# Sliding-window attention and a gated mixture of experts: token blocks of 256 by seven products of quarters in both layers

## The chip, the cores and the metric

The kernel runs on one core of one Trainium2 chip, in fp32. The metric is the time of one execution on the device in microseconds; the number for a kernel is the median of several executions. Matmuls run on TensorE (PE in the profile, its weight loads PEld), elementwise work on VectorE (DVE), ScalarE (ACT) and GpSimd (POOL), and SyncE (SP) issues most of the DMAs.

## What is computed

Eight sequences of 576 tokens pass through attention with eight heads of 64 and a causal window of 64 positions. The heads are joined to rows of 512 numbers, and each of the 4608 rows goes through one of eight experts, a two-layer network with a hidden width of 1024. The expert is the largest of eight gate logits, or the previous token's expert where a local gate says so. Cut to what matters:

```python
scores = np.where(mask, q @ k.T / 8, -1e9)             # mask: 0 <= i - j < 64
x = (softmax(scores) @ v).transpose(0, 2, 1, 3).reshape(B, S, 512)
for b in range(B):
    prev_e = -1
    for s in range(S):
        fresh_e = int(np.argmax(logits[b, s]))
        e = fresh_e if s == 0 or local_gate[b, s] < 0.5 else prev_e
        prev_e = e
        h = np.maximum(x[b, s] @ w1[e], 0.0)             # 512 -> 1024
        out[b, s] = p[e] * (h @ w2[e])                   # 1024 -> 512, p: softmax of the logits
```

## The kernel before, in words

**Attention** (`attention`) works in nine stretches of 512 tokens and four pairs of heads. PE makes the scores and the products with the values, ACT the exponentials, DVE masks them (L276) and divides. Rows go to a DRAM tensor `xs`. The logits come out of the same products.

**The router** (`Router`) sorts tokens by expert into blocks on the chip. `first` handles the first 1728 tokens and fills six whole blocks of 128 tokens while attention still runs; `second` handles everything that is left, 3840 tokens, while those six blocks run. Its tables hold the token of each place (`idx`), its factor (`pw`) and each block's expert (`ej`). Before, the rest is cut into 8 big blocks of 256 tokens, 14 small ones of 128 and 4 half blocks of 64, whose numbers are fixed when the kernel is built; a branch at the end (`more`) handles blocks beyond them.

**The experts** (`Experts`) take one block after the other, in an order that `run` writes out: the six first blocks, then big ones, with a half block after each second one, then the small blocks, and a half block last. For each block:

- `rows` gathers the token rows by an indirect DMA from POOL's queue (L922), `weights` loads both weight matrices of its expert, 2 MB each, from SP's queue (L934). Both are issued two blocks ahead. The weights go into a ring of four buffers (`ring`), and every third block's into two spare ones.
- `turn` transposes the rows on PE (L947) and copies them out of PSUM (L948), on ACT for the six first blocks and on DVE for the rest.
- `hidden` is layer 1: for each of 8 slices of 128 hidden numbers, 4 matmuls with a 128x128 piece of `w1` standing in the array and the block's tokens moving (L962). Each piece of PSUM then goes through a ReLU into `h`, by turns on ACT (L968) and DVE (L966).
- `result` is layer 2: for each 128 tokens, 8 matmuls with a piece of `h` standing and 512 columns of `w2` moving (L992), a copy with the factor on ACT (L997), and an indirect DMA to the output (L998).

On PE the program order is `hidden` of a block, `turn` of the next, `result` of the block. PE's order is written out by hand (`manual_schedule`); the other engines' order in this stage is left to the scheduler. The trace has two records for each fp32 matmul of the program: a big block's layer 1 has 32 matmuls and 64 records.

Of the kernel before, what the change touches and what calls it, by code (L numbers as in the profile page):

```python
# [19 lines left out]
P = 128  # L20
# [26 lines left out]
SMALL = LEFT - NB * BIG  # L47
HF = P // 2
NSM = (SMALL + E * (HF - 1)) // P
SURE = SMALL // P, E // 2  # L50
NBLK = NB + NSM + E
HF0 = SM0 + NSM
NS = HF0 + E
NEG = -1.0e9
SC = 4 * P
NSC = N // SC
# [89 lines left out]
def attention(ctx, tc, ring, q, k, v3, vt, xs, lt, ok, wg2, ident, rt, ex):  # L146
# [49 lines left out]
    col = cp.tile([P, KB, WIN], I32, name="col")  # L196
    nc.gpsimd.iota(col, pattern=[[0, KB], [1, WIN]], base=0, channel_multiplier=0)
    colf = cp.tile([P, KB, WIN], F32, name="colf")
    nc.vector.tensor_copy(colf, col)
    masks = []  # L200
    for i in range(2):
# [322 lines left out]
class Router:  # L524
# [295 lines left out]
    def second(self, psum):  # L820
# [13 lines left out]
        vec.tensor_scalar(bend, bend, float(NB), None, Alu.min)  # L834
        vec.tensor_scalar(boff, boff, float(NB), None, Alu.min)
        vec.tensor_tensor(nb, bend, boff, op=Alu.subtract)

        lim = tl("lim", P, E)
        vec.tensor_scalar(lim, nb, float(BIG), None, Alu.mult)
# [40 lines left out]
        vec.tensor_tensor(pl, pl, self.oh, op=Alu.mult)  # L880
        lo, hi = self.places(pl, CV)
        ej = tabs["ej"]
        self.experts_of(ej[:, :NBLK], NBLK, [(NB, bend), (NSM, send), (E, hend)])
        more = tl("more", 1, 1)
        vec.tensor_scalar(more, hend[0:1, E - 1:], float(SURE[1]), None, Alu.is_gt)
        vec.scalar_tensor_tensor(ej[:, NBLK:], send[0:1, E - 1:], float(SURE[0]), more, Alu.is_gt, Alu.max)
        yield 6.0, False
        at = yield from self.table(psum, slice(0, CV), NS, lo, hi, tabs["idx"], tabs["pw"])

# [2 lines left out]
            vec.tensor_copy(tabs["pwh"][i * HF:(i + 1) * HF], tabs["pw"][:HF, HF0:])  # L892


class Experts:


    def __init__(self, ctx, tc, ring, xs, w1, w2, out, tabs, lt, ident):
        self.tc, self.nc, self.ring, self.spare = tc, tc.nc, ring, None
# [4 lines left out]
    def fetch(self, n, spare=False):  # L904

        st = self.rows({}, n)
        return self.weights(st, n, spare)

    def rows(self, st, n):
        tabs = self.tabs  # L910
        if n < 0:
            idx, pw, rows = tabs["idx1"], tabs["pw1"], T1
            slots = range(-1 - n, -n)
        else:
            idx, pw, rows = tabs["idx"], tabs["pw"], N + 1
            slots = range(2 * n, 2 * n + 2) if n < NB else range(SM0 + n - NB, SM0 + n - NB + 1)
        st.update(x=[], slots=slots, idx=idx, pw=pw, rows=P)
        if n >= NB + NSM:
            st.update(half=n - NB - NSM, rows=HF)
        for s in slots:  # L920
            x = (self.xp if n < 0 else self.xq).tile([P, D], F32, name="xg")
            self.nc.gpsimd.indirect_dma_start(  # L922
                out=x, out_offset=None, in_=self.xs[:rows, :],
                in_offset=bass.IndirectOffsetOnAxis(ap=idx[:, s:s + 1], axis=0))
            st["x"].append(x)
        return st

    def weights(self, st, n, spare=False):
# [12 lines left out]
    def turn(self, st, quiet):  # L941
        nc, n = self.nc, st["rows"]
        st["xt"] = xt = self.wk.tile([P, DK, BIG], F32, name="xt")
        for i, x in enumerate(st["x"]):
            tp = self.ps_t.tile([P, DK, P], F32, name="tp")
            for kk in range(DK):
                nc.tensor.transpose(tp[:, kk, :n], x[:n, kk * P:(kk + 1) * P], self.ident[:n, :n])  # L947
            (nc.scalar.copy if quiet else nc.vector.tensor_copy)(xt[:, :, i * P:i * P + n], tp[:, :, :n])  # L948

    def hidden(self, st, quiet, step):  # L950
        nc = self.nc
        n = len(st["slots"]) * st["rows"]
        st["h"] = h = self.wk.tile([P, FK, BIG], F32, name="h")
        each = 512 // n
        for g in range(FK // each):
            hp = self.ps_h.tile([P, each, n], F32, name="hp")
            for i in range(each):
                m = g * each + i
                for kk in range(DK):
                    for f in range(0, P, st["rows"]):  # L960
                        a = slice(f, f + st["rows"])
                        nc.tensor.matmul(hp[a, i, :], lhsT=st["w1"][:, kk, m * P:(m + 1) * P][:, a],  # L962
                                         rhs=st["xt"][:, kk, :n], start=(kk == 0), stop=(kk == DK - 1))
            o = h[:, g * each:(g + 1) * each, :n]
            if (g % 2 or "half" in st) and not quiet:
                nc.vector.tensor_relu(o, hp)  # L966
            else:
                nc.scalar.activation(o, hp, Act.Relu)  # L968
            step()

    def result(self, st, step):
        nc = self.nc
        if "half" in st:

            s, w = st["half"], D // 2
# [13 lines left out]
        for i, s in enumerate(st["slots"]):  # L989
            yp = self.ps_y.tile([P, D], F32, name="yp")  # L990
            for m in range(FK):
                nc.tensor.matmul(yp, lhsT=st["h"][:, m, i * P:(i + 1) * P], rhs=st["w2"][:, m, :],  # L992
                                 start=(m == 0), stop=(m == FK - 1))
                if m == FK // 2 - 1:
                    step()
            y = self.wk.tile([P, D], F32, name="y")
            nc.scalar.activation(y, yp, Act.Copy, scale=st["pw"][:, s:s + 1])  # L997
            nc.gpsimd.indirect_dma_start(  # L998
                out=self.out[:, :], out_offset=bass.IndirectOffsetOnAxis(ap=st["idx"][:, s:s + 1], axis=0),
                in_=y, in_offset=None, bounds_check=N - 1, oob_is_err=False)  # L1000
            step()

    def space(self, ctx):
        tc = self.tc
        self.spare = ctx.enter_context(tc.tile_pool(name="ex_spare", bufs=2))
# [6 lines left out]
    def run(self, ctx, rt, last=None):  # L1012
# [5 lines left out]
        jobs, late = self.jobs, []  # L1018

        def psum():  # L1020
            return ps_r.tile([P, SC], F32, name="r")

        side = rt.second(psum)

        pause = 0.0

        def step():
# [5 lines left out]
            while side and not trip:  # L1033
                w, trip = next(side, (0.0, None))
                pause += w
                if trip is None:
                    side = None
                    late.append(self.fetch(0, spare=True))

        order = [-1 - n for n in range(FIRST)]  # L1040
        halves = list(range(NB + NSM, NB + NSM + SURE[1]))
        for n in range(NB):
# [4 lines left out]
        total = len(order)  # L1047
        self.turn(jobs[0], True)
        step()
        for i in range(total):  # L1050
            quiet = i < FIRST
            n = order[i + 2] if i + 2 < total else 0
            if n:
                jobs.append(self.fetch(n, spare=n > 0 and (i + 2 - FIRST) % 3 == 0))
            self.hidden(jobs[i], quiet, step)
            if i == FIRST - 1:
                while side:
                    step()
                jobs.insert(FIRST, late[0])
                if last:  # L1060
                    last(psum())
            if i + 1 < total:
                self.turn(jobs[i + 1], quiet)
            self.result(jobs[i], step)

    def more(self, ctx):

        self.space(ctx)
        for i, n in enumerate([*range(NB + SURE[0], NB + NSM), *range(NB + NSM + SURE[1], NBLK)]):
            st = self.fetch(n, spare=i % 3 == 2)  # L1070
# [44 lines left out]
```

## Time and profile before

| | |
|---|---|
| median of three runs | 716.15 us (715.06 to 717.1) |
| the profiled execution's own time | 716.17 us |
| its span, from the first to the last instruction | 714.4 us |
| mean granted TensorE clock | 0.988 |
| PE busy in the span | 667.7 us (93%) |
| DVE busy | 188.5 us (26%) |
| ACT busy | 127.3 us (18%) |
| POOL busy | 117.5 us (16%) |
| first big block starts, last matmul ends | 242.65 us, 705.85 us |

A group's row in the view by lines gives the time in which any of its instructions ran, their mean length, and behind the bar the time in which the engine stood idle before them. Matmuls overlap, so their mean length is longer than the distance between their starts; in the view in order of time, a run's distance is read from the start of one row to the start of the next.

### The profile page before, as it was taken

Reading aid. Unit: us, or ns where it says so; the run is one execution under the profiler, and the core shown is the slowest. Engines: PE = TensorE matmul, PEld = TensorE weight load, DVE = VectorE, ACT = ScalarE, POOL = GpSimd, SP = SyncE. Lnnn points to the kernel's source line nnn. Section 1 sums busy time; section 2 is a strip of 40 time slices with the busy share of each in tenths; the row PEclk is TensorE's granted clock in tenths of the full one; section 3 lists DMA queues with packets and bytes.
Section 4 is the critical chain, followed back from the end, with each engine's and each line's share of the span. In section 5 each row is a group of like instructions: output and inputs, shape, how many; then the busy total and the mean of one; then the engine's idle time right before and its main releaser. Section 6 shows DMA issues by size and latency. Waiting matters only on the chain. (4 is left out here: it accounts for less than half of the span.)

```text
span 714.4 us, 13220 instructions
## 1 busy us (share of the span) xinstructions
PE 667.7 (93%) x5796; PEld 485.8 (68%) x5796; DVE 188.5 (26%) x451; ACT 127.3 (18%) x182; POOL 117.5 (16%) x128
## 2 busy tenths in 40 slices
PE   4888886889999999999999999999999999999994
PEld 2666665776777767585767658676767776677663
DVE  5666896766640010011011001110100001000100
ACT  2655554421111101000010100011001100011000
POOL 4311112211222210112021112101111111010001
PEclk9999999999999999999999999999999999999998
DMA  8999998999879983585567548545988989888700
GB/s 309 388 384 363 393 355 297 401 359 352 325 263 405 407 322 133 205 341 189 227 226 298 197 147 352 214 147 212 327 322 327 323 335 319 327 293 327 266 15 19
DMA packets 37428, 203.85 MB, mean 285 GB/s; under 512 B 3529, under 2 KB 3551, under 8 KB 29168
## 3 DMA queue, kind: packets, MB, share of 16 engines
q1 hardware_dynamic: 28544, 173.45, 65.8%
q0 software_dynamic: 8816, 29.45, 10.4%
q8 instruction: 48, 0.79, 0.4%
q14 instruction: 20, 0.16, 0.1%
HBM read 184.01 MB, written 19.40 MB: 285 GB/s over the span
## 5 line engine op out<-in xcount | busy, mean ns | idle before, releaser
L962 PEld LDWEIGHTS hp<-xt,w 128*128 128x128 f32 (+1 forms) x2304 | 258.3, 179 | 28.9 <-issue 14.7
L962 PE MATMUL hp<-xt,w 128*128 128x128 f32 (+2 forms) x2304 | 274.6, 287 | 1.2 <-ACT xt L948 1.2
L992 PE MATMUL yp<-w,h 128*128 128x512 f32 x576 | 252.7, 593 | 0.0
L992 PEld LDWEIGHTS yp<-w,h 128*128 128x128 f32 x576 | 107.1, 190 | 123.7 <-issue 122.2
L966 DVE TENSOR_SCALAR h<-hp 128x512 f32<-128x512 f32 x34 | 23.5, 691 | 424.8 <-issue 282.8
L998 POOL DMA_INDIRECT out_dram<-y,idx x36 | 37.4, 1040 | 271.9 <-ACT y L997 243.4
L997 ACT ACTIVATE y<-yp,pw 128x512 f32<-128x512 f32 x36 | 24.7, 687 | 317.0 <-PE yp L992 310.7
L922 POOL DMA_INDIRECT xg<-xs,idx x40 | 41.0, 1026 | 193.8 <-PE tp L947 150.6
L257 PE MATMUL sp<-w 64*64 64x128 f32 (+1 forms) x1296 | 48.1, 284 | 14.0 <-DMA w<-in_q_dram 7.2
L257 PEld LDWEIGHTS sp<-w 64*64 64x64 f32 x1296 | 41.5, 146 | 26.6 <-issue 12.0
L286 PE MATMUL xo<-vb,p 128*64 128x74 f32 x576 | 47.9, 236 | 11.3 <-issue 7.2
L276 DVE TENSOR_TENSOR p<-p,mask 128x1024 f32<-128x1024 f32 x36 | 45.9, 1274 | 25.0 <-ACT p L273 25.0
L968 ACT ACTIVATE h<-hp 128x512 f32<-128x512 f32 x42 | 25.1, 597 | 150.7 <-PE hp L962 150.7
L286 PE MATMUL xo<-va,p 128*64 128x74 f32 x576 | 47.7, 236 | 4.1 <-issue 3.5
L286 PEld LDWEIGHTS xo<-vb,p 128*64 128x64 f32 x576 | 41.5, 141 | 13.2 <-issue 6.7
L273 ACT ACTIVATE p<-sp 128x1024 f32<-128x1024 f32 x36 | 36.9, 1025 | 55.4 <-PE sp L257 55.2
L286 PEld LDWEIGHTS xo<-va,p 128*64 128x64 f32 x576 | 41.5, 141 | 7.1 <-issue 6.4
L233 POOL COPY vb<-va 64x1184 f32<-64x1184 f32 x9 | 11.0, 1217 | 93.3 <-PE xo L286 72.5
L295 DVE TENSOR_TENSOR x<-xo,allr 128x512 f32<-128x512 f32 x36 | 24.5, 680 | 0.0
L947 PE MATMUL tp<-ident,xg 128*128 128x128 f32 (+1 forms) x160 | 22.4, 271 | 0.0
L948 DVE COPY xt<-tp 128x512 f32<-128x512 f32 (+1 forms) x32 | 20.1, 647 | 0.0
L947 PEld LDWEIGHTS tp<-ident,xg 128*128 128x128 f32 (+1 forms) x160 | 17.8, 140 | 2.0 <-issue 1.0
(222 smaller groups left out, 235.0 us busy)
## 6 DMA issues: line engine op xcount, KB each, us to landing
w<-in_w_dram SPq DMA_DIRECT2D x64, 2048.0 KB, 9.2
va<-in_v_dram SPq DMA_DIRECT2D x9, 1184.0 KB, 12.7
vtt<-in_vt_dram SPq DMA_DIRECT2D x9, 1024.0 KB, 7.7
xs<-x POOLq DMA_DIRECT2D x9, 1024.0 KB, 10.3
w<-in_k_dram SPq DMA_DIRECT2D x17, 512.0 KB, 11.2
w<-in_q_dram SPq DMA_DIRECT2D x17, 512.0 KB, 12.2
xg<-xs,idx POOLq DMA_INDIRECT x40, 8.9
out_dram<-y,idx POOLq DMA_INDIRECT x36, 8.3
```

The source lines that it names most:

```text
L257: nc.tensor.matmul(sp[c * WIN:(c + 1) * WIN, j, a:b], lhsT=kt[h, hp, block * WIN:(block + 1) * WIN], rhs=qt[h, hp, a:b], start=True, stop= ...
L273: nc.scalar.activation(p, sp, Act.Exp, scale=DH ** -0.5)
L276: nc.vector.tensor_tensor(p, p, m.to_broadcast([P, 2, SC]), op=Alu.mult)
L286: nc.tensor.matmul(xo[par * WIN:(par + 1) * WIN, j, s * VW:(s + 1) * VW], lhsT=p[:, j, b * WIN:(b + 1) * WIN], rhs=w[:, s, 2 * hp + j, :], ...
L295: nc.vector.tensor_tensor(x[:, :, hp].rearrange("p c j d -> p j c d"), o[:, :, :, :DH], rr.to_broadcast([P, 2, 4, DH]), op=Alu.mult)
L922: self.nc.gpsimd.indirect_dma_start(out=x, out_offset=None, in_=self.xs[:rows, :], in_offset=bass.IndirectOffsetOnAxis(ap=idx[:, s:s + 1], ...
L947: nc.tensor.transpose(tp[:, kk, :n], x[:n, kk * P:(kk + 1) * P], self.ident[:n, :n])
L962: nc.tensor.matmul(hp[a, i, :], lhsT=st["w1"][:, kk, m * P:(m + 1) * P][:, a], rhs=st["xt"][:, kk, :n], start=(kk == 0), stop=(kk == DK - 1))
L968: nc.scalar.activation(o, hp, Act.Relu)
L992: nc.tensor.matmul(yp, lhsT=st["h"][:, m, i * P:(i + 1) * P], rhs=st["w2"][:, m, :], start=(m == 0), stop=(m == FK - 1))
L997: nc.scalar.activation(y, yp, Act.Copy, scale=st["pw"][:, s:s + 1])
L998: nc.gpsimd.indirect_dma_start(out=self.out[:, :], out_offset=bass.IndirectOffsetOnAxis(ap=st["idx"][:, s:s + 1], axis=0), in_=y, in_offse ...
```

## The change

Every block of 256 tokens is computed by Strassen's scheme in both layers. A product of two matrices cut in quarters is made of seven products of quarters, or of sums of quarters, in place of eight. `left` makes the four sums of one operand and `right` those of the other, on DVE; `product` is one of the seven, accumulated in PSUM. What two results share stays in PSUM while ACT copies it aside (`keep`), and DVE adds the copy to the finished half (`relu` in layer 1, `put` in layer 2).

- In layer 1 a product is 8 matmuls with 128 moving columns, in place of 32 matmuls with 256 for the whole block; in layer 2 it is 4 matmuls with 256 moving columns, in place of 16 with 512.
- The sums of the weights (`ws1`, `ws2`), of the tokens (`xs`) and of the hidden numbers (`hs`) are made anew for every block, 16 instructions.
- The tokens are cut differently: 13 big blocks, 4 small and 4 half ones. A half or small block follows each second big one; one big, one small and one half block end the order.
- The spare weight buffers go; all weights use the ring of four. `h` has one buffer.
- From the fifth first block on, the order of DVE and ACT is the program's too. The router has to be done one block earlier.
- The router's table has 48 columns in place of 41.

The core of the diff:

```diff
-NB = -(-(LEFT - E * (BIG - 1)) // BIG)
+NB = (LEFT + E * (HF - 1)) // BIG
+SURE = (LEFT + E * HF) // BIG - E // 2, E // 2, E // 2
...
-        self.shifted(nb, cnt, 0, BIG.bit_length() - 1)
+        self.shifted(nb, cnt, HF - 1, BIG.bit_length() - 1)
...
         for name, w, a, b in (("w1", self.w1, DK, F), ("w2", self.w2, FK, D)):
-            t = (self.spare if spare else self.ring).tile([P, a * b], F32, name="w")
+            t = self.ring.tile([P, a * b], F32, name="w")
...
+        if st["big"]:
+            st["xq"] = quarters(xt, DK, BIG)
+            st["xt"] = self.right("xs", st["xq"])
+            w = quarters(st["w1"], DK, F)
+            st["wq"] = [[w[0][0], w[1][0]], [w[0][1], w[1][1]]]
+            st["ws"] = self.left("ws1", st["wq"])
+
+    def left(self, name, a):
+        sub, add = Alu.subtract, Alu.add
+        s1, s2, s3, s4 = self.sums(name, a)
+        for o, x, y, op in ((s1, a[1][0], a[1][1], add), (s2, s1, a[0][0], sub), (s3, a[0][0], a[1][0], sub),
+                            (s4, a[0][1], s2, sub)):
+            self.nc.vector.tensor_tensor(o, x, y, op=op)
+        return s1, s2, s3, s4
...
+    def big_hidden(self, st):
+        a, s, b, t = st["wq"], st["ws"], st["xq"], st["xt"]
+        st["w2q"] = w2 = quarters(st["w2"], FK, D)
+        st["w2t"] = self.right("ws2", w2)
...
+        def product(out, a, b, start=True, stop=True):
+            for m in range(n):
+                for kk in range(DK // 2):
+                    nc.tensor.matmul(out[:, m, :], lhsT=a[:, kk, m * P:(m + 1) * P], rhs=b[:, kk, :],
+                                     start=start and m + kk == 0,
+                                     stop=stop and (m, kk) == (n - 1, DK // 2 - 1), skip_group_check=True)
...
+        product(px, a[0][0], b[0][0], stop=False)
+        u = keep(0, px)
+        product(py, s[0], t[0], stop=False)
+        z = keep(1, py)
+        product(px, s[1], t[1], False, False)
+        v = keep(2, px)
+        product(pz, a[0][1], b[1][0])
+        relu(hq[0][0], pz, u)
+        product(px, s[2], t[2], False, False)
+        relu(hq[1][1], px, z)
+        product(py, s[3], b[1][1], False)
+        relu(hq[0][1], py, v)
+        product(px, a[1][1], t[3], False)
+        relu(hq[1][0], px)
+        st["ha"] = [[hq[0][0], hq[1][0]], [hq[0][1], hq[1][1]]]
+        st["hs"] = self.left("hs", st["ha"])
+
+    def big_result(self, st):
...
+        product(px, a[0][0], b[0][0], stop=False)
+        u = keep(0, px, pw[0])
+        product(py, s[0], t[0], stop=False)
+        z = keep(1, py, pw[1])
+        product(px, s[1], t[1], False, False)
+        v = keep(2, px, pw[0])
+        product(pz, a[0][1], b[1][0])
+        put(0, 0, pz, u)
+        product(px, s[2], t[2], False, False)
+        put(1, 1, px, z)
+        product(py, s[3], b[1][1], False)
+        put(0, 1, py, v)
+        self.scatter(st, 0, y[0])
+        product(px, a[1][1], t[3], False)
+        nc.scalar.activation(y[1][:, :w], px, Act.Copy, scale=pw[1])
+        self.scatter(st, 1, y[1])
...
+        small = list(range(NB, NB + SURE[1]))
+        half = list(range(NB + E, NB + E + SURE[2]))
+        between = half[1:] + small
+        for n in range(SURE[0]):
             order.append(n)
-            if n % 2 and len(halves) > 1:
-                order.append(halves.pop(0))
-        order += list(range(NB, NB + SURE[0])) + halves
+            if n % 2 and between:
+                order.append(between.pop(0))
+        order += between + half[:1]
```

On PE, where the big blocks begin, the program before has one row for each layer of a block (`hp` is layer 1's PSUM tile, `yp` layer 2's, `tp` that of the transposes of the next block's rows `xg`; `64x64` rows are a half block):

```order
L962 MATMUL hp<-xt,w 128x256 x32
L947 MATMUL tp<-ident,xg 128x128 x8
L992 MATMUL yp<-w,h 128x512 x16
L962 MATMUL hp<-xt,w 128x256 x32
L947 MATMUL tp<-ident,xg 128x64 x4
L992 MATMUL yp<-w,h 128x512 x16
L962 MATMUL hp<-xt,w 64x64 x64
L947 MATMUL tp<-ident,xg 128x128 x8
L979 MATMUL yp<-w,h 64x256 x16
```

After, the first big block at the same place on PE (`xs` and `ws` are the sums of tokens and weights, `hs` those of the hidden numbers; both layers' PSUM tiles are called `hp`):

```order
L998 MATMUL hp<-xt,w 128x128 x8
L998 MATMUL hp<-xs,ws_2840 128x128 x16
L998 MATMUL hp<-xt,w 128x128 x8
L998 MATMUL hp<-xs,ws_2840 128x128 x8
L998 MATMUL hp<-xt,ws_2840 128x128 x8
L998 MATMUL hp<-xs,w 128x128 x8
L947 MATMUL tp<-ident,xg 128x128 x8
L1041 MATMUL hp<-w,h 128x256 x4
L1041 MATMUL hp<-ws_2868,hs 128x256 x8
L1041 MATMUL hp<-w,h 128x256 x4
L1041 MATMUL hp<-ws_2868,hs 128x256 x4
L1041 MATMUL hp<-w,hs 128x256 x4
```

Layer 1 is now 56 matmuls with 128 columns, and layer 2 is 28 with 256, the seventh product following the last row. Five of the seven products read a sum.

DVE in the same place before, where each pair of ReLUs belongs to one big block and the copies to the next block's transposed rows:

```order
L966 TENSOR_SCALAR h<-hp 128x512 x2
L948 COPY xt<-tp 128x4x128 x2
L966 TENSOR_SCALAR h<-hp 128x512 x2
L948 COPY xt<-tp 128x4x64
L966 TENSOR_SCALAR h<-hp 128x8x64
```

DVE after, between the two layers of the first big block, with the rows of the second one being prepared (`kept` are ACT's copies of layer 2, `y` the rows for the output):

```order
L948 COPY xt<-tp 128x4x128 x2
L971 TENSOR_TENSOR xs<-xt 128x256
L971 TENSOR_TENSOR xs<-xt,xs 128x256
L971 TENSOR_TENSOR xs<-xt 128x256
L971 TENSOR_TENSOR xs<-xt,xs 128x256
L963 TENSOR_TENSOR ws_2969<-w 128x1024
L963 TENSOR_TENSOR ws_2969<-ws_2969,w 128x1024
L963 TENSOR_TENSOR ws_2969<-w 128x1024
L963 TENSOR_TENSOR ws_2969<-w,ws_2969 128x1024
L1050 SCALAR_TENSOR_TENSOR y<-hp,pw,kept_2983 128x256
L1050 SCALAR_TENSOR_TENSOR y<-hp,pw,kept_2989 128x256
L1050 SCALAR_TENSOR_TENSOR y<-hp,pw,kept_2995 128x256
```

The sums for the next block's first layer now stand on DVE ahead of the three instructions that finish this block's second layer. After these rows come four more weight sums (128x1024), three additions and four sums of hidden numbers (128x512 each).

More of the change, by code (lines that the diff above doesn't have):

```diff
@@ L892, in second, with quarters @@
             vec.tensor_copy(tabs["pwh"][i * HF:(i + 1) * HF], tabs["pw"][:HF, HF0:])
+def quarters(t, rows, cols):
+    r, c = rows // 2, cols // 2
+    return [[t[:, i * r:(i + 1) * r, j * c:(j + 1) * c] for j in range(2)] for i in range(2)]
 class Experts:
     def __init__(self, ctx, tc, ring, xs, w1, w2, out, tabs, lt, ident):
-        self.tc, self.nc, self.ring, self.spare = tc, tc.nc, ring, None
+        self.tc, self.nc, self.ring = tc, tc.nc, ring
         self.xs, self.w1, self.w2, self.out, self.tabs, self.ident = xs, w1, w2, out, tabs, ident
@@ L916, in rows @@
             slots = range(2 * n, 2 * n + 2) if n < NB else range(SM0 + n - NB, SM0 + n - NB + 1)
-        st.update(x=[], slots=slots, idx=idx, pw=pw, rows=P)
-        if n >= NB + NSM:
-            st.update(half=n - NB - NSM, rows=HF)
+        st.update(x=[], slots=slots, idx=idx, pw=pw, rows=P, big=len(slots) == 2)
+        if n >= NB + E:
+            st.update(half=n - NB - E, rows=HF)
         for s in slots:
@@ new lines, in big_result, with product, keep, put @@
+    def big_result(self, st):
+        nc = self.nc
+        a, s, b, t = st["ha"], st["hs"], st["w2q"], st["w2t"]
+        w = D // 2
+        px, py, pz = (self.ps_h.tile([P, D], F32, name="hp")[:, :w] for _ in range(3))
+        pw = [st["pw"][:, i:i + 1] for i in st["slots"]]
+        y = [self.wk.tile([P, D], F32, name="y") for _ in range(2)]
+        def product(out, a, b, start=True, stop=True):
+            for m in range(FK // 2):
+                nc.tensor.matmul(out, lhsT=a[:, m, :], rhs=b[:, m, :], start=start and m == 0,
+                                 stop=stop and m == FK // 2 - 1, skip_group_check=True)
+        def keep(i, x, pw):
+            o = self.one.tile([P, w], F32, name=f"kept{i}")
+            nc.scalar.activation(o, x, Act.Copy, scale=pw)
+            return o
+        def put(i, j, x, y2):
+            nc.vector.scalar_tensor_tensor(y[i][:, j * w:(j + 1) * w], x, pw[i], y2, Alu.mult, Alu.add)
+        product(px, a[0][0], b[0][0], stop=False)
[14 more added lines that the diff above has]
+        self.scatter(st, 1, y[1])
@@ L950, in hidden, with scatter @@
+    def scatter(self, st, i, y):
+        s = st["slots"][i]
+        self.nc.gpsimd.indirect_dma_start(
+            out=self.out[:, :], out_offset=bass.IndirectOffsetOnAxis(ap=st["idx"][:, s:s + 1], axis=0),
+            in_=y, in_offset=None, bounds_check=N - 1, oob_is_err=False)
     def hidden(self, st, quiet, step):
         nc = self.nc
-        n = len(st["slots"]) * st["rows"]
-        st["h"] = h = self.wk.tile([P, FK, BIG], F32, name="h")
+        if st["big"]:
+            return self.big_hidden(st)
+        n = st["rows"]
+        st["h"] = h = self.wk.tile([P, FK, BIG], F32, name="h", bufs=1)
@@ L988, in result @@
             return
[L989 to L1001, printed above, removed]
+        yp = self.ps_y.tile([P, D], F32, name="yp")
+        for m in range(FK):
+            nc.tensor.matmul(yp, lhsT=st["h"][:, m, :P], rhs=st["w2"][:, m, :], start=(m == 0), stop=(m == FK - 1))
+            if m == FK // 2 - 1:
+                step()
+        y = self.wk.tile([P, D], F32, name="y")
+        nc.scalar.activation(y, yp, Act.Copy, scale=st["pw"][:, st["slots"][0]:st["slots"][0] + 1])
+        self.scatter(st, 0, y)
+        step()
     def space(self, ctx):
         tc = self.tc
-        self.spare = ctx.enter_context(tc.tile_pool(name="ex_spare", bufs=2))
+        self.one = ctx.enter_context(tc.tile_pool(name="ex_one", bufs=1))
         self.xq = ctx.enter_context(tc.tile_pool(name="ex_xq", bufs=6))
```

79 lines of the change are left out of this document (46 added, 33 removed).

## The prediction

> **What bounds the kernel now.** I read the page's busy times first, then the groups by line with shapes kept apart, then PE in order of time, then the stage's window, and last the rows of DVE, POOL and the DMA queue that have to price the new work.
>
> ```profile
> PE 667.7 (93%) x5796; PEld 485.8 (68%) x5796; DVE 188.5 (26%) x451; ACT 127.3 (18%) x182; POOL 117.5 (16%) x128
> ...
> L992 PE MATMUL yp<-w,h 128*128 128x512 f32 x576 | 252.7, 593 | 0.0
> ...
> L962 PE MATMUL hp<-xt,w 128*128 128x128 f32 x1280 | 146.7, 275 | 1.2 <-ACT xt L948 1.2
> L962 PE MATMUL hp<-xt,w 128*128 128x256 f32 x512 | 112.1, 380 | 0.0
> ```
>
> PE does nearly all of the work and almost never waits in the experts' stage: the idle time ahead of its three large groups is 1.2 us in all. From the first big block to the last matmul nothing else counts:
>
> ```profile
> core 0: us, PE busy (x) PEld busy (x) DVE busy (x) ACT busy (x) POOL busy (x), PEclk, DMA share, GB/s
> 242.65:705.85 463.20, 462.35 (x2657) 325.24 (x2655) 41.55 (x66) 40.65 (x64) 59.54 (x60) 1.00 0.69 254
> ```
>
> PE is busy for 462.35 of 463.20 us at a granted clock of 1.00, DVE for 41.55 us. So a shorter PE program shortens this stage one for one, until an engine that now idles is late. In PE's order of time:
>
> ```profile
> 213.20 7.31 PE L962 MATMUL hp<-xt,w 128*128 128x128 f32 x64
> 220.34 0.60 PE L947 MATMUL tp<-ident,xg 128*128 128x128 f32 x4
> 220.78 7.03 PE L992 MATMUL yp<-w,h 128*128 128x512 f32 x16
> ...
> 242.65 13.98 PE L962 MATMUL hp<-xt,w 128*128 128x256 f32 x64
> 256.46 1.04 PE L947 MATMUL tp<-ident,xg 128*128 128x128 f32 x8
> 257.33 13.90 PE L992 MATMUL yp<-w,h 128*128 128x512 f32 x32
> 271.07 13.98 PE L962 MATMUL hp<-xt,w 128*128 128x256 f32 x64
> 284.98 0.46 PE L947 MATMUL tp<-ident,xg 64*128 64x64 f32 x4
> 285.36 14.00 PE L992 MATMUL yp<-w,h 128*128 128x512 f32 x32
> 299.29 3.95 PE L962 MATMUL hp<-xt,w 128*64 128x64 f32 x128
> 303.18 1.09 PE L947 MATMUL tp<-ident,xg 128*128 128x128 f32 x8
> 304.20 3.67 PE L979 MATMUL yp<-w,h 128*64 128x256 f32 x32
> 307.80 14.08 PE L962 MATMUL hp<-xt,w 128*128 128x256 f32 x64
> ...
> 494.84 7.31 PE L962 MATMUL hp<-xt,w 128*128 128x128 f32 x64
> ...
> 509.29 7.31 PE L962 MATMUL hp<-xt,w 128*128 128x128 f32 x64
> ```
>
> From start to start: a record with 128 moving columns takes 7.14/64 = 0.1116 us, one with 256 takes 13.81/64 = 0.2158, one with 512 takes 13.74/32 = 0.429. The time goes nearly with the columns; halving 256 costs 3%. A big block takes 28.42, a small one 14.45, a half one 8.51; the transposes 0.87 for two rows of 128, 0.44 for one, 0.38 for a half block.
>
> **The change on PE.** Seven products of layer 1 are 112 records of 128 columns, 112 x 0.1116 = 12.50 us (now 13.81). Seven of layer 2 are 56 records of 256 columns, 56 x 0.2158 = 12.08 (now 13.74). Thirteen blocks: 13 x 24.58 = 319.6. Transposes: 12 x 0.87 + 4 x 0.44 + 4 x 0.38 = 13.7. Four small blocks without theirs: 4 x 14.01 = 56.0. Four half blocks without theirs (8.51 less 1.02): 4 x 7.49 = 30.0, and 0.9 for the bare wait at the end, where the last half block has nothing to cover its ReLU, as now. Together 420.2 us in place of 463.2: 43.0 less. Both cuts have the same number of places (8 x 256 + 14 x 128 and 13 x 256 + 4 x 128 are both 3840), so no token's work leaves PE in another way.
>
> Against this rule of proportion stands the Trainium skill, "TensorE: Matmul & The Clock Gate", section on the back-to-back issue gap: sustained, a matmul of 128 columns takes about 81 ns and one of 512 about 131, so narrow ones cost well over their columns. By that ratio four of 128 would cost 2.5 times one of 512, and cutting widths in half would eat the eighth that is saved. This trace disagrees for fp32: 4 x 0.1116 against 0.429 is 4% more. I take the rows.
>
> **The change on DVE.** The prices:
>
> ```profile
> 42.27 1.23 DVE L276 TENSOR_TENSOR p<-p,mask 128x1024 f32<-128x1024 f32 x1 [1.97 <-ACT p L273]
> 43.42 0.20 DVE L291 RECIPROCAL allr<-xo 128x8 f32<-128x8 f32 x1
> ...
> 129.63 1.20 DVE L276 TENSOR_TENSOR p<-p,mask 128x1024 f32<-128x1024 f32 x1
> ...
> 131.13 0.68 DVE L295 TENSOR_TENSOR x<-xo,allr 128x512 f32<-128x512 f32 x1
> ...
> 172.27 0.35 DVE L691 TENSOR_TENSOR base<-base,start 128x184 f32<-128x184 f32 x1
> ...
> 180.07 0.47 DVE L880 TENSOR_TENSOR pl<-pl,oh 128x296 f32<-128x296 f32 x1
> ...
> 257.27 1.28 DVE L948 COPY xt<-tp 128x512 f32<-128x512 f32 x2
> ...
> 246.36 0.60 ACT L968 ACTIVATE h<-hp 128x512 f32<-128x512 f32 x1 [2.78 <-PE hp L962]
> ```
>
> A sum over 1024 columns is L276's row, 1.23, over 512 is L295's 0.68, and over 256 lies between 184 (0.35) and 296 (0.47), 0.42. A big block has 8 of the first (9.84), 7 of the second (four `hs`, three additions: 4.76), 7 of the third (four `xs`, three `put`: 2.94) and two copies (1.28): 18.8 us, beside 25.5 of PE. DVE has room, but its order makes a chain. Take a big block followed by a big one, in us from its first matmul. PE's products of layer 1 end at 1.8, 3.6, 5.4, 7.1, 8.9, 10.7 and 12.5. DVE makes `ws2` until 4.9, adds after the fourth, fifth and sixth product, the last from 10.8 to 11.5; ACT's ReLU ends at 12.2; `hs` runs to about 15.0, the copies to 16.3, `xs` to 18.0, the next block's `ws1` to 22.9, the first two `put` to 23.8. PE has transposed by 13.4 and does layer 2 in steps of 1.73: the sixth product ends at 23.7, and the seventh overwrites the PSUM tile that the second `put` reads. With 0.1 for the signal PE waits 0.2. In the same way the first product that needs `hs`, at 15.1, finds it made at 13.0, and the next block finds its `ws1` whole.
>
> After a half block, DVE starts the next block's copies at 4.9 us of the half block's 8.5, has `ws1` whole at 12.5 and `ws2` at 17.4, and adds behind the fourth and fifth product until 18.8, where PE's seventh wants the PSUM tile at 19.2: no wait. So the waits cost six times 0.2, say 1.3 us. The cover is thin: if every DVE instruction took 10% more, the chain from `hs` to `put` would grow by 1.0, six such places and six more behind half and small blocks at up to 0.9, 6 to 12 us.
>
> **Weights.**
>
> ```profile
> w<-in_w_dram SPq DMA_DIRECT2D x64, 2048.0 KB, 9.2
> ```
>
> With the spare buffers gone, `w2` of a block behind a half block can start only when the big block ahead of that is finished, and DVE now needs it when `ws1` is made, 12.5 us later, in place of at layer 2. A load lands in 9.2. Elsewhere the distance is a whole block. I cost it at nothing, covered by 3.3 us.
>
> **The rest.** The table's matmuls grow from 205 to 240 columns, 37 of them, which I bound by 0 and 0.5 us and take 0.5, as PE issues them on the path. The router's last tables are written on PE ahead of the second half of the fourth first block's layer 2 in both programs, so its earlier due time holds nobody. Gathers and scatters keep their number of rows and run two blocks ahead. ACT gets seven copies and four ReLUs per big block, 0.60 each by the row at 246.36, under 7 us of 25.
>
> **Sum.** 43.0 less, 1.3 and 0.5 back: 41.2. The profiled execution took 716.17 us (span 714.4), within 0.02 of the median, so 675.0.
>
> **The rivals.**
>
> *DVE becomes the bound, and the kernel slower.* An instruction of DVE with two operands in SBUF can be held up by POOL:
>
> ```profile
> 106.81 2.19 DVE L276 TENSOR_TENSOR p<-p,mask 128x1024 f32<-128x1024 f32 x1
> ...
> 107.86 2.16 POOL L237 COPY vb<-va 64x1184 f32<-64x1184 f32 x1
> ...
> 129.40 1.06 POOL L922 DMA_INDIRECT xg<-xs,idx  x1 [0.98 <-DVE idx L783]
> ```
>
> Beside POOL's copy the same instruction took 2.19. The Trainium skill, "SBUF — State Buffer", on who interferes with whom, has this rule: a DVE instruction with two SBUF inputs contends with a GpSimd instruction that reads SBUF, and the loser waits for the whole of the other. If POOL's gathers did that to all sums, stretched by 1.6 to 1.9, DVE would need 18.8 x 1.6 = 30 us a block and set the pace: at least 4.5 us a block over PE's 25.5, 13 x 4.5 = 59, so 734 or more. It decides from 28.7 us a block (25.5 and 41.2/13), sums 1.5 times as long. Against it: the row at 129.63 ran inside POOL's gather at 129.40 and took 1.20, and the new stage has gathers and scatters on POOL, no copies. Chance 0.05.
>
> *Narrow products cost more than their columns.* PE could lose a fixed time with each short run, fourteen of them a block, each behind a signal of another engine. In the rows above, a run of 16 records of L992 and one of 32 have the same 0.429, so a border there is free, but those signals came early. At 0.1 a product it would be 13 x 14 x 0.1 = 18: 693. It is here that the rule of the page on TensorE would show, of which these rows bear out 3 to 4%. Chance 0.11.
>
> *Weights come late.* If `w2` landed after 15 us in place of 9.2, the three blocks behind half blocks would wait 2.5 each, and as much again if the rest of the ring is pushed back: 683 to 690. Chance 0.08.
>
> *The cut doesn't fit the tokens.* More than 13, 4 and 4 blocks would run the branch at the end, at over 25 us a block. Counted from the reference, the tokens left per expert are 521, 371, 617, 421, 433, 222, 530 and 725, which make 13, 4 and 4. Chance 0.01.
>
> **How the numbers follow.** The forecast, 675.0, keeps 0.75. Its own ends are 671 (no waits, free borders, somewhat less at the joints) and 687 (DVE 10% slower). The range adds the borders' rival: 670 to 693. A difference of 0.3%, 2.1 us, is about what can be told from none. Faster by more than that: 0.75 + 0.11 + 0.08 = 0.94; slower: 0.05; the same: 0.01.
>
> **What would show it.** Big blocks of 25 to 26 us from start to start, PE's idle time small and put down to DVE `y` before a block's last product; the 1024-column sums at 1.2 to 1.3 us and DVE near 75% busy in the stage; records of 128 and 256 columns 0.112 and 0.216 us apart. I am wrong if PE waits for `hs` or `ws` in every block, if the sums take 1.5 us or more, if DVE waits for `w`, or if PE loses time at each product without waiting for anything.

## The result, and the profile after

The kernel after takes 683.68 us (median of four, 683.29 to 684.88), the kernel before beside it 715.61 us (713.86 to 717.1): a ratio of 0.9558, with a 95% interval of 0.9532 to 0.9583. The forecast was 675.0 in a range of 670 to 693: the gain came, but 8.7 us of it are missing. The profiled execution took 683.29 us, its span is 681.5.

The first view is that by stretches of time, cut where PE's work changes: attention's end, the first hidden matmul, the first big block, the last matmul. This is the kernel before:

```profile
core 0: us, PE busy (x) PEld busy (x) DVE busy (x) ACT busy (x) POOL busy (x), PEclk, DMA share, GB/s
0.00:148.90 148.90, 112.81 (x2584) 92.00 (x2584) 108.92 (x265) 71.08 (x91) 37.12 (x50) 0.95 0.97 358
148.90:150.13 1.23, 0.01 (x2) 0.03 (x1) 1.13 (x4) 0.59 (x1) 0.13 (x1) 1.00 1.18 480
150.13:242.65 92.52, 92.52 (x557) 68.56 (x558) 36.88 (x117) 14.55 (x25) 19.71 (x17) 1.00 0.92 349
...
705.85:714.40 8.55, 0.00 (x0) 0.00 (x0) 0.00 (x0) 0.47 (x1) 0.98 (x1) 0.78 0.04 12
```

And the same stretches of the kernel after:

```profile
0.00:145.10 145.10, 110.11 (x2584) 90.03 (x2584) 109.80 (x265) 70.92 (x91) 36.23 (x50) 0.96 1.00 374
145.10:157.74 12.64, 0.01 (x2) 0.00 (x1) 4.59 (x18) 0.94 (x2) 0.79 (x1) 0.60 0.78 320
157.74:252.38 94.64, 94.64 (x556) 70.44 (x557) 40.10 (x108) 14.05 (x24) 17.92 (x16) 0.98 0.76 286
252.38:675.08 422.70, 421.82 (x3273) 379.26 (x3271) 236.66 (x319) 87.04 (x155) 69.92 (x60) 1.00 0.62 231
675.08:681.50 6.42, 0.00 (x1) 0.00 (x0) 0.00 (x0) 0.47 (x1) 0.98 (x1) 0.89 0.05 12
```

The fourth row answers to the 463.20 us of the prediction's first window: 422.70 us, 40.5 less, at a granted clock of 1.00 and with PE idle for 0.9 us of it. The loss is in the second row. Between attention's last matmul and the first hidden one lay 1.23 us; now there are 12.64, in which PE does nothing. Added up, the span changes by -3.8 (attention), +11.4 (that gap), +2.1 (the six first blocks), -40.5 (big, small and half blocks) and -2.1 (the end): -32.9 us, which is 714.4 less 681.5.

In PE's order of time, the big block at 252.38 and what follows it:

```profile
252.38 1.95 PE L998 MATMUL hp<-xt,w 128*128 128x128 f32 x16
254.16 3.74 PE L998 MATMUL hp<-xs,ws 128*128 128x128 f32 x32
...
276.12 1.89 PE L1041 MATMUL hp<-ws,h 128*128 128x256 f32 x8
277.85 1.95 PE L998 MATMUL hp<-xt,w 128*128 128x128 f32 x16
...
303.12 3.95 PE L1089 MATMUL hp<-xt,w 128*64 128x64 f32 x128
...
311.63 2.05 PE L998 MATMUL hp<-xt,w 128*128 128x128 f32 x16
...
337.20 1.95 PE L998 MATMUL hp<-xt,w 128*128 128x128 f32 x16
```

From start to start a big block takes 277.85 - 252.38 = 25.47 us (forecast 25.45), the half block 311.63 - 303.12 = 8.51 as before. The first product's 16 records take 1.78 us, 0.111 each; the seventh product of layer 2 has 8 in 1.73, 0.216 each. DVE in the same block, at the joint where the prediction put PE's only wait:

```profile
270.02 1.22 DVE L963 TENSOR_TENSOR ws<-w 128x1024 f32<-128x1024 f32 x1
271.27 1.22 DVE L963 TENSOR_TENSOR ws<-ws,w 128x1024 f32<-128x1024 f32 x1
272.41 1.22 DVE L963 TENSOR_TENSOR ws<-w 128x1024 f32<-128x1024 f32 x1
273.55 1.22 DVE L963 TENSOR_TENSOR ws<-w,ws 128x1024 f32<-128x1024 f32 x1
274.68 0.87 DVE L1050 SCALAR_TENSOR_TENSOR y<-hp,pw,kept 128x256 f32<-128x256 f32 x2
```

The sums take 1.22 us as priced, but three of the four steps from start to start are 1.13 to 1.14. The pair of `put` ends at 275.55, ahead of PE's seventh product at 276.12. So PE waits for no `put` at all.

Now the gap. The rows of PE, ACT and POOL at attention's end, from the three engines' views in order of time (what stands in brackets is the idle time before, and who ended it):

```profile
142.93 0.66 PE L947 MATMUL tp<-ident,xg 128*128 128x128 f32 x4
...
144.89 0.23 PE L284 MATMUL xo<-va,p 128*64 128x74 f32 x1
157.74 5.52 PE L1089 MATMUL hp<-xt,w 128*128 128x128 f32 x32 [12.63 <-ACT xt L948]
163.10 0.38 PE L625 MATMUL r<-ident,vk 128*23 128x128 f32 x2
...
157.10 0.58 ACT L948 COPY xt<-tp 128x512 f32<-128x512 f32 x1 [8.68 <-DMA xs<-x]
...
146.66 0.79 POOL L352 DMA_DIRECT2D xs<-x  x1 [1.78 <-DVE x L293]
```

PE waits for the first block's transposed tokens `xt`; ACT's copy that writes them waits for the DMA that stores attention's last rows, `xs<-x`, which POOL issues at 146.66. The copy reads nothing of that DMA: it reads `tp`, which PE had made from 142.93 on, before attention ended. That leaves the place as what the two share: the DMA would read rows that lie where `xt` is to be written, which the first two experiments test. The change opens a new pool for sums and copies, `ex_one` (53 KB a partition), where the spare weight buffers (32 KB) were opened, ahead of the working pool that holds `xt`; so everything behind it moves by 21 KB. By the diff, two constants of 2 KB each also leave attention's pool ahead of `x`, the tile that the DMA reads, which makes 25 KB between `xt` and `x`.

The gap has an aftermath. The 32 records of the first row take 163.10 - 157.74 = 5.36 us from start to next start. The view by stretches tells why:

```profile
157.74:159.00 1.26, 1.26 (x6) 1.26 (x7) 0.00 (x0) 0.00 (x0) 0.00 (x0) 0.50 0.00 0
...
161.00:162.00 1.00, 1.00 (x10) 1.00 (x10) 0.00 (x0) 0.00 (x0) 0.00 (x0) 0.85 0.06 16
```

After the idle time the granted clock is 0.50 for more than 3 us, which costs about 1.7 us. The Trainium skill, "TensorE: Matmul & The Clock Gate", Part 1, has that rule: an idle window of about 3.4 us halves PE's clock until as long a busy one has passed. The trace agrees: the clock comes back in the slice from 161 to 162, 3.3 to 4.3 us after the first matmul. For waits close to that length the runs below are less tidy.

### The profile page after: what moved, and what is told of

The parts are those of the page before. It is cut to its first block, busy times and chain, and to the rows that moved or that the text cites. A ratio compares the mean times of both kernels' runs of the same rounds, so it can differ in the third digit from the quotient of the medians.

```text
span 681.5 us, 14905 instructions
## 1 busy us (share of the span) xinstructions
PE 626.6 (92%) x6412; PEld 539.7 (79%) x6412; DVE 391.1 (57%) x709; ACT 173.4 (25%) x273; POOL 125.8 (18%) x128
## 5 line engine op out<-in xcount | busy, mean ns | idle before, releaser
L1089 PE MATMUL hp<-xt,w 128*128 128x128 f32 (+1 forms) x1152 | 91.4, 254 | 12.7 <-ACT xt L948 12.6
L1089 PEld LDWEIGHTS hp<-xt,w 128*128 128x128 f32 (+1 forms) x1152 | 90.0, 170 | 16.2 <-ACT xt L948 12.8
L998 PE MATMUL hp<-xs,ws 128*128 128x128 f32 x624 | 73.9, 275 | 0.0
L998 PEld LDWEIGHTS hp<-xs,ws 128*128 128x128 f32 x624 | 71.8, 192 | 0.0
L1041 PE MATMUL hp<-ws,hs 128*128 128x256 f32 x312 | 71.6, 379 | 0.0
L1120 PE MATMUL yp<-w,h 128*128 128x512 f32 x160 | 70.9, 594 | 0.0
L1041 PEld LDWEIGHTS hp<-ws,hs 128*128 128x128 f32 x312 | 59.3, 190 | 8.1
L274 DVE TENSOR_TENSOR p<-p,mask 128x1024 f32<-128x1024 f32 x36 | 45.9, 1276 | 21.6 <-ACT p L271 21.5
L1120 PEld LDWEIGHTS yp<-w,h 128*128 128x128 f32 x160 | 29.5, 190 | 32.6 <-issue 31.8
L998 PE MATMUL hp<-xt,w 128*128 128x128 f32 x416 | 51.0, 276 | 0.0
L1041 PE MATMUL hp<-w,h 128*128 128x256 f32 x208 | 49.5, 381 | 0.0
```

The lines of the kernel that those rows point to most:

```text
L274: nc.vector.tensor_tensor(p, p, m.to_broadcast([P, 2, SC]), op=Alu.mult)
L998: nc.tensor.matmul(out[:, m, :], lhsT=a[:, kk, m * P:(m + 1) * P], rhs=b[:, kk, :], start=start and m + kk == 0, stop=stop and (m, kk) == ...
L1041: nc.tensor.matmul(out, lhsT=a[:, m, :], rhs=b[:, m, :], start=start and m == 0, stop=stop and m == FK // 2 - 1, skip_group_check=True)
L1120: nc.tensor.matmul(yp, lhsT=st["h"][:, m, :P], rhs=st["w2"][:, m, :], start=(m == 0), stop=(m == FK - 1))
```

## The experiments

In these kernels "the stage" is the time from the first big block's first matmul to the end of the last matmul: 463.20 us before, 422.70 after.

### Where the new pool lies

`one_last` is the kernel after with two lines swapped:

```diff
     def space(self, ctx):
         tc = self.tc
-        self.one = ctx.enter_context(tc.tile_pool(name="ex_one", bufs=1))
         self.xq = ctx.enter_context(tc.tile_pool(name="ex_xq", bufs=6))
         self.wk = ctx.enter_context(tc.tile_pool(name="ex_work", bufs=2))
+        self.one = ctx.enter_context(tc.tile_pool(name="ex_one", bufs=1))
```

> The changed kernel with one edit: the pool of the sums is placed in SBUF behind the pool that holds the transposed tokens, in place of ahead of it. Theory A, that the transposed tokens lie on the attention's output rows and so wait for the DMA that reads them: PE's wait of 12.6 us ahead of the first block falls to 1 to 2 us, the first big block starts 8 to 12 us earlier, and the time falls from 683.7 to 671 to 676. Theory B, that the first block is late for its gathered rows or for its weights: the wait stays, under another releaser, and the time stays at 683 to 685. The stage of the big blocks, 422.7 us, is the same in both.

Measured: 671.06 us (670.45 to 673.95); against the kernel before, 713.62 beside it, 0.9421 (0.9378 to 0.9465). The stretches of `one_last`, from attention's end on:

```profile
145.60:146.78 1.18, 0.00 (x1) 0.03 (x1) 1.14 (x4) 0.58 (x1) 0.00 (x0) 1.00 1.04 434
146.78:239.71 92.93, 92.93 (x557) 68.72 (x557) 43.48 (x123) 14.41 (x25) 18.55 (x17) 1.00 0.88 332
239.71:662.10 422.39, 421.54 (x3273) 379.07 (x3271) 236.62 (x319) 87.04 (x155) 68.80 (x60) 1.00 0.62 231
```

The gap is 1.18 us again, the six first blocks are 1.7 us shorter at a clock of 1.00, and the stage is the same to 0.3 us. No instruction was changed. This version is faster than both kernels.

`before_shift` is the other direction: the kernel before, nothing of Strassen's scheme in it, with one unused tile behind the spare buffers.

```diff
         self.spare = ctx.enter_context(tc.tile_pool(name="ex_spare", bufs=2))
+        pad = ctx.enter_context(tc.tile_pool(name="ex_pad", bufs=1)).tile([P, 25 * 256], F32, name="pad")
```

> The kernel before, nothing of the change in it, with an unused pool of 25 KB a partition opened behind the spare buffers, so that the first transposed tokens xt lie on the rows x of attention's output, as in the kernel after. Theory A (it is the place in SBUF that made TensorE wait 12.6 us in the kernel after): TensorE waits 10 to 13 us ahead of the first of the six blocks, its clock is lower behind the wait, and time is 8 to 15 us above the kernel before's. Theory B (the wait came from VectorE's or ACT's new order in the change): within 2 us of the kernel before. The output is the reference's.

Measured: 725.13 us (724.7 to 728.79), against 713.14 for the kernel before: 1.017 (1.012 to 1.022), 12.0 us more. The same view of `before_shift`:

```profile
146.15:158.83 12.68, 0.00 (x0) 0.00 (x0) 4.59 (x18) 0.94 (x2) 0.80 (x1) 0.60 0.78 320
158.83:252.98 94.15, 94.15 (x556) 70.19 (x557) 33.47 (x102) 14.19 (x24) 19.03 (x16) 0.98 0.79 297
252.98:716.18 463.20, 462.35 (x2657) 325.24 (x2655) 41.52 (x66) 40.65 (x64) 59.46 (x60) 1.00 0.68 254
```

12.68 us of gap and a clock of 0.60 in it, as in the kernel after, and the stage's 463.20 us of before. An unused tile alone makes a loss of this size, without the new order of DVE and ACT and without the router's earlier due time, and `one_last` loses nothing with both of them.

### What each part of the change gives

`recut` has the change's cut of the tokens, its order, its four weight buffers, and plain products in all blocks (the condition in `turn` becomes `if False`, and `hidden` and `result` don't branch to the new functions). `layer1` has the seven products in layer 1 alone, `layer2` in layer 2 alone. All three have the pools as in `one_last`.

```diff
-        if st["big"]:
-            return self.big_hidden(st)      # recut, layer2
...
-        if st["big"]:
-            return self.big_result(st)      # recut, layer1
```

> The new cut (13 big, 4 small, 4 half blocks), the ring of four and the program's order, but every big block with plain products, without any sums; the pools as in the run before. If the gain is the seven products' alone, the stage from the first big block to the last matmul takes 463 us as in the kernel before, and the time is 714 to 718. If the new cut itself saved time on PE (fewer and larger blocks), the stage would be shorter than 460.

> Seven products in layer 1 only, layer 2 plain. By the rows a big block's layer 1 falls from 13.81 to 12.50 us, 17.0 us for thirteen: a stage of 446 us and a time of 697 to 701. If narrow products lost a fixed time each, layer 1 would show it first, with its runs of 16 records: a stage of 450 or more.

> Seven products in layer 2 only, layer 1 plain. By the rows a big block's layer 2 falls from 13.74 to 12.08 us, 21.6 us for thirteen: a stage of 441.5 us and a time of 692 to 697. The hidden numbers' sums now stand right between the two layers, with the last ReLU of layer 1 ahead of them, so a wait of PE of up to 1 us a block may show, 13 us in all, if DVE's order makes the chain the bound.

| kernel | median us | ratio to before (95%) | stage us |
|---|---|---|---|
| `recut` | 707.96 | 0.9925 (0.9894 to 0.9957) | 460.82 |
| `layer1` | 693.45 | 0.9733 (0.967 to 0.9797) | 443.80 |
| `layer2` | 687.92 | 0.9652 (0.9597 to 0.9707) | 439.42 |
| `one_last` | 671.06 | 0.9421 (0.9378 to 0.9465) | 422.39 |

The stages come from these rows, of `recut`, `layer1` and `layer2`:

```profile
237.70:698.52 460.82, 459.97 (x2337) 314.36 (x2335) 41.53 (x66) 40.63 (x64) 59.42 (x60) 1.00 0.57 211
```

```profile
241.18:684.98 443.80, 442.95 (x2961) 319.79 (x2959) 125.86 (x176) 80.32 (x129) 61.77 (x60) 1.00 0.58 220
```

```profile
238.71:678.13 439.42, 438.57 (x2649) 373.62 (x2647) 151.04 (x206) 47.46 (x90) 63.83 (x60) 1.00 0.59 222
```

Layer 1 gives 460.82 - 443.80 = 17.0 us, layer 2 gives 21.4, and both together 38.43: the sum, to 0.01. By the prediction's prices they are 13 x (13.81 - 12.50) = 17.0 and 13 x (13.74 - 12.08) = 21.6. The cut itself gives 2.4: five more big blocks replace ten small ones, whose records of 128 columns cost 3% more than those of 256. Only these stages are compared so closely; the medians also depend on where attention ends, which is the next point.

`before_cols` asks whether attention's earlier end, 143.3 to 146.8 us in these kernels and 144.9 in the kernel after against 148.7 before, is the change's doing, by the one edit of the change in attention:

```diff
-    col = cp.tile([P, KB, WIN], I32, name="col")
+    cols = pp.tile([P, 2, SC], F32, name="p").rearrange("p i (b q) -> p i b q", q=WIN)
+    col, colf = cols[:, 0].bitcast(I32), cols[:, 1]
     nc.gpsimd.iota(col, pattern=[[0, KB], [1, WIN]], base=0, channel_multiplier=0)
-    colf = cp.tile([P, KB, WIN], F32, name="colf")
```

> The kernel before with only that edit of the change that lays col and colf into a buffer of the pool of p. In the traces so far attention's last matmul stands at 148.69 us in the kernel before and at 143.3 to 146.8 in the kernels with the change's other form. Theory A (the edit, or the cut's smaller constants, moves attention's start or end): attention's last matmul at 143 to 146 and time 2 to 5 us below the kernel before. Theory B (attention's end differs from run to run by some microseconds): no difference that can be measured, within 2 us. The output is the reference's.

Measured: 712.66 us against 713.14, 0.9991 (0.9968 to 1.0014): no difference. Attention's last matmul starts at 145.74 here, and at 145.92 in `before_shift`, which has no edit in attention at all. `recut` and `layer1` do the same work in this stretch and end it 3.5 us apart, at 143.3 and 146.8. So the 3.8 us between the two profiled executions are no more than the spread of a stretch in which the DMA share is 0.95 to 1.00, and nothing shows them to be part of the change's gain; the same 2 to 3 us lie between the kernel before's 716.15 us and the 713 of later executions.

### How much room VectorE has

`ws1_twice` is `one_last` with the sums of `ws1` made twice over:

```diff
             st["ws"] = self.left("ws1", st["wq"])
+            self.left("ws1", st["wq"])
```

> The kernel one_last (671.06 us) with the four sums of ws1 made twice over for every big block: 4 x 1.14 = 4.6 us more VectorE work ahead of the puts, in front of TensorE's seventh product of layer 2. Theory A (VectorE's cover in the big blocks is thin: in one_last the pair of puts that the seventh product needs ends 0.6 us before TensorE comes to it): the puts end some 4.6 us later, TensorE waits 4 to 5 us in each big block that follows a big or a small one, and time is 700 to 712 us. Theory B (VectorE's load decides: 18.8 + 4.6 = 23.4 us a big block, still under TensorE's 25.5): within 3 us of one_last. The output is the reference's.

Measured: 721.99 us (719.86 to 723.3), 1.0107 of the kernel before (1.0061 to 1.0153): 51 us more than `one_last`, and 1% more than the kernel without Strassen's scheme: the whole gain is gone. What PE waited for in the stage, and its view by stretches:

```profile
PE hp L1042 <- DVE y L1051: 22.6, 6, 4.1
PE hp L999 <- DVE ws L964: 9.0, 3, 3.0
```

```profile
240.09:713.56 473.47, 439.91 (x3273) 391.11 (x3271) 296.38 (x371) 86.82 (x155) 73.33 (x60) 0.97 0.55 206
```

DVE is busy for 296 of 473 us, 63%, and PE waits all the same: six times for `put` (up to 4.1 us), three times for `ws` (3.0 each). So theory A holds in kind, and load doesn't decide. The forecast of 700 to 712 was too low by a second effect. PE is idle for 33.6 us of the stage, 32.7 more than in `one_last`, but the same 3273 records are also busy for 18.4 us longer, at a clock of 0.97. PE in order of time behind one such wait:

```profile
336.52 3.78 PE L1042 MATMUL hp<-ws,h 128*128 128x256 f32 x8 [3.66 <-DVE y L1051]
340.10 3.21 PE L999 MATMUL hp<-xt,w 128*128 128x128 f32 x16
343.14 3.74 PE L999 MATMUL hp<-xs,ws 128*128 128x128 f32 x32
```

After 3.66 us of waiting, 8 records take 3.58 us in place of 1.73, and the next 16 take 3.04 in place of 1.79: 3.1 us lost on top of the wait, at a granted clock of 0.50 until some 6 us after it. The six waits for `put` don't all cost the same: one of 3.71 us loses 3.1 too, the other four, of 3.71 to 4.10, lose 1.5 to 1.8 each, 12.7 in all. Nor does the length of a wait settle it. These are two waits for `ws` behind a half block:

```profile
310.21 3.81 PE L999 MATMUL hp<-xs,ws 128*128 128x128 f32 x32 [3.00 <-DVE ws L964]
313.85 1.95 PE L999 MATMUL hp<-xt,w 128*128 128x128 f32 x16
...
380.21 5.44 PE L999 MATMUL hp<-xs,ws 128*128 128x128 f32 x32 [3.02 <-DVE ws L964]
385.48 1.95 PE L999 MATMUL hp<-xt,w 128*128 128x128 f32 x16
```

The first 32 records take 313.85 - 310.21 = 3.64 us, near the 3.57 of a run without a wait; the second take 5.27, at a clock of 0.50 from 381 to 383, and lose 1.7. The third such wait, of 3.02 as well, loses nothing. With 12.7 and 1.7, 14.4 of the 18.4 us lie in records slowed behind a wait; the other 4 were not traced one by one.

`pool_beside` is `one_last` with copies on POOL beside the sums:

```diff
             st["ws"] = self.left("ws1", st["wq"])
+            for i in range(4):
+                c = self.wk.tile([P, 1024], F32, name="beside", bufs=1)
+                self.nc.gpsimd.tensor_copy(c, st["w1"][:, i, :])
```

> The kernel one_last with four copies of 128x1024 on POOL, into a tile that nobody reads, put beside the sums of ws1 of every big block. Theory A (the rival of the prediction: a POOL copy holds up VectorE's two-input instructions, as in the row of the kernel before that took 2.19 instead of 1.20 us; the change escaped it only because its POOL does gathers and scatters there): the sums of 1024 that lie beside a copy take 1.8 to 2.3 us, at least four a big block, VectorE is 3 to 5 us late at the puts and time is 690 to 715 us. Theory B (POOL's copies don't matter to it): sums stay at 1.22 us and time within 3 us of one_last's 671. The output is the reference's.

Measured: 679.93 us (679.05 to 680.42), 8.9 more than `one_last`. POOL's copies start as soon as POOL comes to them, and in a block behind a half block that is beside the sums of the hidden numbers, `hs`. Rows of DVE and POOL there:

```profile
310.76 2.21 DVE L966 TENSOR_TENSOR hs<-h 128x512 f32<-128x512 f32 x1 [0.69 <-ACT h L1013]
313.01 1.41 DVE L966 TENSOR_TENSOR hs<-hs,h 128x512 f32<-128x512 f32 x1
314.35 1.52 DVE L966 TENSOR_TENSOR hs<-h 128x512 f32<-128x512 f32 x1
315.79 1.52 DVE L966 TENSOR_TENSOR hs<-h,hs 128x512 f32<-128x512 f32 x1
...
311.35 5.41 POOL L958 COPY beside<-w 128x1024 f32<-128x1024 f32 x4
```

Four sums that take 0.69 us each elsewhere take 6.7 together, and PE's seventh product then waits 3.24 us for its `put`. Two of the three such waits:

```profile
325.60 1.99 PE L1044 MATMUL hp<-ws,h 128*128 128x256 f32 x8 [3.24 <-DVE y L1053]
...
388.51 3.23 PE L1044 MATMUL hp<-ws,h 128*128 128x256 f32 x8 [3.29 <-DVE y L1053]
391.53 2.43 PE L1001 MATMUL hp<-xt,w 128*128 128x128 f32 x16
393.79 3.74 PE L1001 MATMUL hp<-xs,ws 128*128 128x128 f32 x32
```

Behind the first no clock is lost, behind the second 1.8 us: 3.02 and 2.26 from start to start in place of 1.73 and 1.79. Theory A holds in kind, and its size was too large (690 to 715 was expected): DVE's busy time in the stage grew by only 14.4 us (251.04 against 236.62 in the view by stretches), and PE's waits are 7.7 us in all. In the kernel after, with gathers and scatters alone on POOL, the sums run undisturbed. Its groups in the stage, by form:

```profile
L971 DVE TENSOR_TENSOR ws<-w 128x1024 f32<-128x1024 f32 x26 | 31.7, 1219 | 6.7 <-PE hp L1041 6.7
L963 DVE TENSOR_TENSOR hs<-h 128x512 f32<-128x512 f32 x26 | 17.9, 688 | 9.0 <-ACT h L1010 9.0
```

## Why the prediction was right and where it was wrong

- **PE's sum: right.** 420.2 us were forecast for the stage, 421.82 of PE's time and 0.9 of waiting were measured. Both layers' parts came out at 17.0 and 21.4 us against 17.0 and 21.6. The 2.5 us over lie around the half blocks: the big block ahead of one takes 25.27 us (277.85 to 303.12) where the prices make 24.96, the half one 8.51 in place of 8.36, the big one behind it 25.57 (311.63 to 337.20) in place of 25.45, three times over; the last small block and the half block behind it are 0.3 and 0.4 longer.
- **Narrow products cost more than their columns: no.** 0.111 us for 128 columns and 0.216 for 256, in runs of 8 and 16 records behind signals of three engines. The rows decided rightly; the ratio of 2.5 that the prediction works out from the Trainium skill, "TensorE: Matmul & The Clock Gate", section on the back-to-back issue gap, did not show.
- **DVE's prices: right; its waits: too high by 1.3 us.** 1.22, 0.69 and 0.42 us against 1.23, 0.68 and 0.42. Adding up lengths put the second `put` at 23.8 us after the block's start; it ended at 23.2 (275.55 - 252.38), since a sum that doesn't read the one right before it starts 1.14 us after it. "DVE near 75% busy in the stage" was worked out wrongly: 18.8 of 25.5 us holds for a big block alone, and over the whole stage it was 236.66 of 422.70, 56%.
- **"The cover is thin": shown.** 4.6 us more work for DVE in a block cost 51 us. The prediction's 6 to 12 us for a DVE that is 10% slower, with waits of up to 1.0 us, was not tested: where waits reach 3 to 4 us, as here, the lower clock behind them comes on top.
- **DVE bound by POOL: not in this kernel, but the mechanism is there.** `pool_beside` shows sums of 0.69 us that take 1.4 to 2.2 beside POOL's copies. The prediction's row at 129.63 ran mostly, not wholly, inside the gather, which ends at 130.46.
- **Weights late: no.** PE waited for nothing but the 0.8 us of the last half block's ReLU between 252 and 676 us.
- **The cut fits the tokens: yes.** No matmul stands behind the last half block, so the branch for further blocks didn't run.
- **The router's larger table: right.** 92.93 us for the six first blocks in `one_last` against 92.52, 0.4 for the 0.5 taken.
- **The step that failed** is the part called "The rest", which put all that changes ahead of the stage at 0.5 us: the prediction summed what each engine executes in the stage and took for granted that everything ahead of it stays, "the rest" being tables, gathers and ACT's copies. The new pool shifted the working tiles onto rows that a DMA was still reading; that cost 11.4 us of waiting and 1.7 of clock, 13.1 in all. `one_last` got back 13.2 in those two stretches (12.64 + 94.64 against 1.18 + 92.93) and 12.6 of the median; `before_shift` loses 12.0 with nothing but the shift. With attention's end (-3.8) and the shorter end after the last matmul (-2.1), which are not shown to be the change's doing, the 8.3 us by which the span misses the forecast are complete: 11.4 + 1.6 + 1.2 - 3.8 - 2.1, where 1.6 is the first blocks beyond the 0.5 and 1.2 the stage beyond 421.5.
- **That the time lies between 670 and 693 is partly luck.** The upper part of the range stood for losses at the borders of products and for a slower DVE, and neither came. What took the room was a term that the sum doesn't have.

What is left open: how much of the shorter end is the change's. Behind the last matmul lie 6.4 to 7.2 us in the kernels with the new cut, 8.55 in the kernel before and 7.2 in `before_shift`, which end with the same half block.

## What to carry to other kernels

A new pool is also a change of addresses: before adding up what a change executes, look at what lies under the first tile of each pool behind it, and whether a DMA still reads or writes there when that tile is made; put new pools last, where their first use is late. For a scheme that trades TensorE's work for VectorE's, the load of VectorE says little (56% here, and 63% was already too slow): follow the chain of one block and see by how many tenths of a microsecond its last link is ahead. And a wait of TensorE of 3.7 us or more cost more than itself every time here, one of 3.0 to 3.3 us two times in five.

## What the runs showed of the hardware that was not expected

- PE's clock: idle for 12.6 us, then a granted clock of 0.50 for 3.3 to 4.3 us, a loss of 1.7 us; after six waits of 3.66 to 4.10 us a loss of 1.5 to 3.1 us each; after five of 3.00 to 3.29 us none three times (3.00, 3.02, 3.24) and 1.7 to 1.8 us twice (3.02, 3.29). So the length of the wait alone doesn't tell.
- Sums of 1024 columns on DVE last 1.22 us each, but one that doesn't read the sum right before it starts 1.14 us after that one, before it has ended (271.27 to 272.41); one that reads it starts 1.25 after it (270.02 to 271.27).
- Copies of 1024 columns on POOL stretched sums of 512 columns on DVE from 0.69 to 1.41 to 2.21 us; a sum of 1024 columns that ran while POOL issued a scatter (253.82, the scatter from 253.54 to 254.68 in the kernel after) kept its 1.23 us.
